# Two max tiles of a pair in one tile of two PSUM banks, reduced by one VectorE instruction, in the lead of an attention and token-mixing kernel

## The chip, the cores and the metric

The kernel runs on one core of one Trainium2 chip. The metric is device time in microseconds (us) for one execution. TensorE (PE) multiplies matrices into PSUM, which has eight banks; a bank holds 512 float32 values in each of 128 partitions, and one matmul writes within one bank. VectorE (DVE) and ScalarE (ACT) read the banks, GpSimd (POOL) works on on-chip memory, and SyncE (SP) issues the DMAs. Each engine runs its own queue in order; semaphores make one wait for another.

## The reference

A gate mixes two branches over the same input `x` (2048 tokens, 640 channels). Branch A is attention with 32 heads of 20 channels that share one key and one value head. Branch B is an MLP over the token axis with a hidden width of 1728.

```python
g = sigmoid((x * gate_w).sum(-1, keepdims=True))

# A: q has 32 heads, k and v have one
q = (x @ wq).reshape(B, S, H, Dh).transpose(0, 2, 1, 3)
k, v = x @ wk, x @ wv
p = softmax(einsum("bhqd,bkd->bhqk", q, k) * Dh ** -0.5)
a = einsum("bhqk,bkd->bhqd", p, v).transpose(0, 2, 1, 3).reshape(B, S, H * Dh) @ wo

# B: MLP over tokens
h = layernorm(x)
u = gelu(einsum("bsd,sf->bdf", h, w1) + b1)
b = (einsum("bdf,fs->bds", u, w2) + b2).transpose(0, 2, 1)

out = g * a + (1 - g) * b
```

## The kernel before

[...]

The softmax needs each row's maximum before its exponentials. So the scores are computed twice. A **max tile** (made by `ms_next`) is a 128x512 block of scores with the queries on the partitions; VectorE reduces it to one maximum per query (L500). A **score tile** (made by `qk`, called by `s_next`) is the transposed block, with the keys on the partitions; its query operand carries the row maxima as extra rows, and ScalarE takes the exponential (L652). Attention output is then collected by `pv_group` (L754). The work comes in 32 groups `n` of four heads and 512 queries. A group has 64 max tiles, 32 for each half `b` of the rows of TensorE's array. The two halves can work at the same time, on different banks.

After a first stage (projections, layer norm) comes the **lead**, the stretch that the change edits: `for fc in range(PRO)` with seven chunks of the MLP's first product. A chunk has 16 steps, and a step has six matmuls, three for each half (L686), into the two accumulators `pu`. `lead()` puts a pair of max tiles, one for each half, behind 45 of the first 106 steps. After 32 pairs, half of the 64 needed, `ms_done` takes the maxima of the group (L515), POOL negates and splits them (L517 to L519), and `store_max` and `fetch_max` turn them and send them through DRAM to the query operand. In the last chunk the numbers in `FIRST_S` name four steps behind which a first pair stands: one max tile (half 0) and one of the first four score tiles (half 1). At the end of each chunk `gelu` reads one accumulator with ScalarE (L548) and, some steps later, adds the other with VectorE (L555).

The order of instructions is written out by hand, engine by engine (`manual_schedule`), so a Python call stands where its instruction stands in its engine's queue. In the lead, banks are used in turn: `lead_bank` rotates the four banks `ms` x3 and `g`. The accumulators use `s` x2 for even chunks, and the third `s` and `o` for odd ones.

The **main stage** follows (`main`). There a small planner picks the order of tiles: each bank in `pool` has a time at which it is taken to be free, `FREE_AT` for the first ones, and `bank_take` picks the earliest. The remaining chunks of the MLP (L1035 and others) run beside max and score tiles and go to the bank `g`.

Of the kernel before, what the change touches and what calls it, by code (L numbers as in the profile page):

```python
# [17 lines left out]
P = 128  # L18
# [15 lines left out]
SIXES = range(3)  # L34
LAST_M = 2
M_FIRST = 1
FIRST_S = (4, 7, 10, 13)
NP = 12
EPS = 1e-5
GC = math.sqrt(2.0 / math.pi)  # L40
# [4 lines left out]
def mix_kernel(ctx: ExitStack, tc: tile.TileContext, A_x, A_wq, A_wk, A_wv, A_wo,  # L45
# [436 lines left out]
    def ms_next(b):  # L482
        k = given[b]
        if k >= 32 * NU:
            return None
        given[b] += 1
        n, r = divmod(k, 32)
        (kq, pr), qt = divmod(r // 4, 2), r % 4

        def step():  # L490
            if n not in mtiles:
                mtiles[n] = mpool.tile([P, 16, 4], F32, name="mp")
            ms = lead_bank() if lead_banks else bank_take()
            nc.tensor.matmul(ms, qmax[n][64 * b:64 * b + 60, pr, qt * P:(qt + 1) * P],  # L494
                             kst[64 * b:64 * b + 60, kq * NB:(kq + 1) * NB], start=True, stop=True)
            if not lead_banks:
# [3 lines left out]
            r = nc.vector.tensor_reduce(mtiles[n][:, c, kq:kq + 1], ms, axis=AX.X, op=ALU.max)  # L500
            if behind is not None:
                tc.add_manual_dep(r.ins, behind.ins.name, SYNC, reason="row tiles that share a bank")
                last["sig"] = r
            issued[b] += 1
            if min(issued) == 32 * n + 1:
                new_qmax(n + 1)

        return step

    def ms_done():  # L510
        n = len(row_max)
# [21 lines left out]
            nc.sync.dma_start(out=rows.rearrange("j p q -> j (p q)"), in_=src[b])  # L533

    chain, ahead = [], []
    lead_banks = []

    def lead_bank():
        lead_banks.append(lead_banks.pop(0))
        return lead_banks[-1]  # L540


    def gelu(d, fc, accs):
# [92 lines left out]
    def qk(u, pr, b):  # L636
        n, kb = units[u]
        assert n in back_in
        if kb == 4 and pr == 0 and b == 0:
            new_q(n + 1)  # L640
        q = qtiles[n]
        s = lead_bank() if lead_banks else bank_take()
        nc.tensor.matmul(s, kst[64 * b:64 * b + 62, kb * P:(kb + 1) * P], q[64 * b:64 * b + 62, pr, :],  # L643
                         start=True, stop=True)
        ready[u] = 0.0 if lead_banks else max(ready.get(u, 0.0), bank_give(s, "exp"))
        p = next_p()
        ptiles[u, 2 * pr + b] = p

        behind, last["ins"] = last["ins"], None

        def exp():
            e = nc.scalar.activation(p, s, AF.Exp, scale=SCALE)  # L652
# [12 lines left out]
    lead_banks.extend((*tiles[:3], ps_g.tile([P, NB], F32, name="g")))  # L665
    at, skip, final = 0, 3, NS * PRO - 6
    one_by_one[0] = True

    def lead():
        for b in range(2):  # L670
            ms_next(b)()
        ms_done()

    for fc in range(PRO):
        pu = tiles[3 + 2 * (fc % 2):5 + 2 * (fc % 2)]
        for hf in range(4):
            w1_upto(4 * fc + hf + 4)
            for f in [q_parts_due.pop(0) for _ in range(min(len(q_parts_due), 1 + fc // 5))] if fc else []:
# [142 lines left out]
    def b2_jobs(st):  # L821
        hold = {}

        def mm(fc, k, d, half):
            if not hold.get("n"):
                hold["p"], hold["n"] = ps_g.tile([P, NB], F32, name="g"), 0
# [126 lines left out]
    def a_jobs(st):  # L953
# [9 lines left out]

        def mm(c, k, d, half):
            if not hold.get("n"):
                hold["p"], hold["n"] = ps_g.tile([P, NB], F32, name="g"), 0
# [54 lines left out]
    def b1_jobs(d, fc):  # L1021
# [5 lines left out]

        def mm(st, k, half):
            if not hold.get("n"):
                hold["p"], hold["n"] = ps_g.tile([P, NB], F32, name="g"), 0  # L1030
            wh, wl = w1t[base + st // HS]
            w, h = ((wh, h_hi), (wh, h_lo), (wl, h_hi))[k]
            hold["n"] += 1
# [181 lines left out]
    spare[0] = True  # L1215
    ring[:0] = extra_p

    pool.append((lanes[0], ps_g.tile([P, NB], F32, name="g")))
    begin = lanes[0]
    while later:  # L1220
        f = later.pop(0)[1]
# [149 lines left out]
```

## Time and profile before

| what | value |
|---|---|
| median of 3 runs | 1612.38 us (1612.14 to 1612.48) |
| the profiled execution | 1611.67 us |
| span of its core | 1609.9 us |
| granted TensorE clock | 1.0 |
| TensorE busy | 1603.3 us |
| VectorE busy | 1356.4 us |
| ScalarE busy | 1309.3 us |
| POOL busy | 869.6 us |
| the lead, first to last L686 matmul | 96.4 to 159.7 us |

A row of the timeline gives the start in us from the span's start, the time taken, the engine, the line, the operation, the tile written and the tiles read, the shapes, and how many instructions were merged into the row. Matmuls are pipelined, so that TensorE looks busy while it goes slowly; the count of matmuls in a window tells more than the busy time. PE and PEld are TensorE's multiplications and its weight loads.

### The profile page before, as it was taken

How to read it: one execution, taken by the hardware profiler on the slowest of the kernel's cores; microseconds unless marked ns; L12 is line 12 of the kernel's file. 1: busy time of each engine (PE TensorE's matmuls, PEld its weight loads, DVE VectorE, ACT ScalarE, POOL GpSimd, SP SyncE). 2: the span in 40 equal slices, each digit the busy share in tenths (PEclk: the TensorE clock that was granted, in tenths of full speed). 3: DMA queues.
4: the chain of work that ended last, by engine and by line, in shares of the span. 5: the costliest groups of instructions: out<-in, count | busy, mean ns of one | idle time of the engine just before them, and what ended most of it. 6: DMA issues, size and time to landing. Idle time of an engine off the chain costs nothing.

```text
span 1609.9 us, 39500 instructions
## 1 busy us (share of the span) xinstructions
PE 1603.3 (100%) x14865; PEld 1121.9 (70%) x14865; DVE 1356.4 (84%) x2344; ACT 1309.3 (81%) x2565; POOL 869.6 (54%) x977
## 2 busy tenths in 40 slices
PE   9999999999999999999999999999999999999998
PEld 7889776677767776666666666666666666666676
DVE  6689999999999999888888888888888888766643
ACT  4545888888888888888888888888888888999974
POOL 6568766778867777644544434454544333344420
PEclk9999999999999999999999999999999999999999
DMA  7755223223233323222222122222222112245531
GB/s 215 213 164 143 78 72 81 75 76 88 75 88 84 76 64 89 64 73 81 73 69 66 54 64 70 69 73 81 73 73 69 54 51 68 87 122 180 157 95 55
DMA packets 183750, 145.07 MB, mean 90 GB/s; under 512 B 38291, under 2 KB 145424, under 8 KB 183560
## 3 DMA queue, kind: packets, MB, share of 16 engines
q1 hardware_dynamic: 183272, 142.23, 31.3%
q8 instruction: 117, 1.92, 0.5%
q14 instruction: 73, 0.60, 0.1%
q10 hardware_dynamic: 288, 0.33, 0.1%
HBM read 108.75 MB, written 32.15 MB: 88 GB/s over the span
## 4 chain that ended last, share of the span: by engine, by line
PE 98%; DVE 1%; POOL 0%; issue 0%; ACT 0%; DVEq 0%; POOLq 0%
PE s L754 16%; PE g L832 12%; PE s L643 10%; PE ms L754 10%; PE g L1035 9%; PE ms L643 8%; PE ms L494 7%; PE s L494 5%; PE pp L303 4%; PE o L754 4%; PE o L643 3%; PE o L494 2%; PE s L686 2%; PE g L971 2%; DVE mp L500 1%; PE s L926 1%
## 5 line engine op out<-in xcount | busy, mean ns | idle before, releaser
L500 DVE TENSOR_REDUCE mp<-ms 128x1 f32<-128x512 f32 x965 | 631.7, 680 | 57.6 <-PE ms L494 43.2
L652 ACT ACTIVATE p<-s 128x512 f32<-128x512 f32 x938 | 542.4, 615 | 45.4 <-PE ms L754 12.8
L500 DVE TENSOR_REDUCE mp<-s 128x1 f32<-128x512 f32 x755 | 499.4, 681 | 74.5 <-PE s L494 52.7
L652 ACT ACTIVATE p<-ms 128x512 f32<-128x512 f32 x820 | 482.2, 612 | 31.3 <-PE s L754 13.5
L767 POOL TENSOR_TENSOR acc<-acc,part 128x512 f32<-128x512 f32 x213 | 275.4, 1293 | 309.9 <-ACT part L766 297.8
L494 PE MATMUL ms<-kst,qmx 60*128 60x512 f32 x965 | 378.2, 412 | 0.1
L643 PE MATMUL s<-qst,kst 62*128 62x512 f32 x944 | 362.7, 408 | 0.2 <-DVE mp L500 0.2
L643 PE MATMUL ms<-qst,kst 62*128 62x512 f32 x826 | 323.9, 406 | 0.1
L1035 PE MATMUL g<-slot,wh 64*128 64x320 f32 x1344 | 306.0, 312 | 0.0
L494 PE MATMUL s<-kst,qmx 60*128 60x512 f32 x755 | 301.5, 413 | 0.0
L754 PE MATMUL s<-p,v_sb 128*32 128x512 f32 x2240 | 269.3, 598 | 0.0
L1035 PEld LDWEIGHTS g<-slot,wh 64*128 64x128 f32 x1344 | 216.4, 184 | 69.6 <-issue 49.5
L500 DVE TENSOR_REDUCE mp<-o 128x1 f32<-128x512 f32 x303 | 206.3, 681 | 42.8 <-PE o L494 36.9
L134 POOL TENSOR_TENSOR wl<-wr,wh 128x512 fp32r<-128x512 f32 (+1 forms) x176 | 218.3, 1240 | 30.5 <-ACT wh L131 15.4
L643 PEld LDWEIGHTS s<-qst,kst 62*128 62x128 f32 x944 | 173.3, 185 | 60.7 <-ACT p L652 27.1
L1035 PE MATMUL g<-slot,wl 64*128 64x320 f32 x672 | 205.2, 305 | 0.0
L832 PE MATMUL g<-u,wh 64*128 64x320 f32 x864 | 196.4, 309 | 0.0
L832 PE MATMUL g<-slot,wh 64*128 64x320 f32 x864 | 196.3, 309 | 0.0
L643 PEld LDWEIGHTS ms<-qst,kst 62*128 62x128 f32 x826 | 152.6, 185 | 43.8 <-ACT p L652 29.4
L494 PEld LDWEIGHTS ms<-kst,qmx 60*128 60x128 f32 x965 | 175.1, 185 | 4.2 <-DVE mp L500 0.4
L652 ACT ACTIVATE p<-o 128x512 f32<-128x512 f32 x264 | 162.3, 615 | 11.3 <-PE ms L754 7.1
L754 PE MATMUL ms<-p,v_sb 128*32 128x512 f32 x1344 | 161.6, 598 | 0.0
(251 smaller groups left out, 3081.3 us busy)
## 6 DMA issues: line engine op xcount, KB each, us to landing
wr<-in_B_w_dram SPq DMA_DIRECT2D x136, 256.0 KB
qmx<-q_scr SPq DMA_DIRECT2D x192, 80.0 KB
qst<-q_scr SPq DMA_DIRECT2D x192, 80.0 KB
ot<-l_scr SPq DMA_DIRECT2D x120, 64.0 KB
y_scr<-yo SPq DMA_DIRECT2D x16, 320.0 KB
slot<-o_scr SPq DMA_DIRECT2D x16, 320.0 KB
o_scr<-ot SPq DMA_DIRECT2D x124, 40.0 KB
o_scr<-acc SPq DMA_DIRECT2D x124, 40.0 KB
```

The costliest lines, as they stand in the source:

```text
L134: nc.gpsimd.tensor_sub(wl[:, :nv], wr[:, :nv], f32(wh[:, :nv]))
L303: nc.tensor.matmul(pp, w, t, start=first and n == 0, stop=not more and n == len(steps) - 1)
L494: nc.tensor.matmul(ms, qmax[n][64 * b:64 * b + 60, pr, qt * P:(qt + 1) * P], kst[64 * b:64 * b + 60, kq * NB:(kq + 1) * NB], start=True, s ...
L500: r = nc.vector.tensor_reduce(mtiles[n][:, c, kq:kq + 1], ms, axis=AX.X, op=ALU.max)
L643: nc.tensor.matmul(s, kst[64 * b:64 * b + 62, kb * P:(kb + 1) * P], q[64 * b:64 * b + 62, pr, :], start=True, stop=True)
L652: e = nc.scalar.activation(p, s, AF.Exp, scale=SCALE)
L686: nc.tensor.matmul(pu[r][:, :HD2], w[rows, c, :], h[rows, st, :], start=(st == 0 and k == 0), stop=(st == NS - 1 and k == 2))
L754: nc.tensor.matmul(o[32 * hh:32 * hh + 32, :], v_sb[:, kb + i, :], ptiles.pop((u, hh)), start=opened and i == 0, stop=(i == len(us) - 1) a ...
L767: nc.gpsimd.tensor_add(sums[0], sums[0], part)
L832: other_tile(half, nc.tensor.matmul(hold["p"][:, :HD2], w[r, i, :], u[d][r, fc, :], start=(hold["n"] == 1), stop=(hold["n"] == 6 * FC - 3)))
L971: other_tile(half, nc.tensor.matmul(hold["p"][:, :HD2], o[r, c, :], w[r, c, d * HD2:(d + 1) * HD2], start=(hold["n"] == 1), stop=(hold["n" ...
L1035: other_tile(half, nc.tensor.matmul(hold["p"][:, :HD2], w[r, st % HS, :], h[d][r, st, :], start=(hold["n"] == 1), stop=(hold["n"] == 6 * NS)))
```

## The change

In the lead, the four rotating banks become two tiles of two banks each, taken in turn from a pool `ps_l`. `ms_pair` replaces the two calls of `ms_next`: it issues both matmuls of a pair into the two halves of such a tile, and one VectorE instruction reduces 128x2x512 values to two maxima per partition, which it writes 32 columns apart. The pool is closed at the end of the lead, and the banks `ms` x3 and `o` are made from its four banks for the main stage.

The four first pairs no longer share the rotation. Their max tiles all use the third `s` bank, their score tiles the bank `g`, and they stand behind steps 6, 9, 12 and 15 of the last chunk instead of 4, 7, 10 and 13. The accumulators of odd chunks are the third `s` and `g` instead of the third `s` and `o`. `FREE_AT` has new numbers for the new banks.

```diff
-FIRST_S = (4, 7, 10, 13)
+FIRST_S = (6, 9, 12, 15)
...
-            ms = lead_bank() if lead_banks else bank_take()
+            ms = lead_bank() if ps_l else bank_take()
...
+    def ms_pair():
+        n = given[0] // 32
+        assert n == given[1] // 32
+        if n not in mtiles:
+            mtiles[n] = mpool.tile([P, 16, 4], F32, name="mp")
+        ms = ps_l[0].tile([P, 2, NB], F32, name="ms")
+        at = []
+        for b in range(2):
+            (kq, pr), qt = divmod(given[b] % 32 // 4, 2), given[b] % 4
+            nc.tensor.matmul(ms[:, b, :], qmax[n][64 * b:64 * b + 60, pr, qt * P:(qt + 1) * P],
+                             kst[64 * b:64 * b + 60, kq * NB:(kq + 1) * NB], start=True, stop=True)
+            at.append(((2 * b + pr) * 4 + qt) * 4 + kq)
+            given[b] += 1
+        out = mtiles[n].rearrange("p c k -> p (c k)")[:, at[0]:at[1] + 1:at[1] - at[0]]
+        nc.vector.tensor_reduce(out, ms, axis=AX.X, op=ALU.max)
+        for b in range(2):
+            issued[b] += 1
+        if min(issued) == 32 * n + 1:
+            new_qmax(n + 1)
...
-    ps_m = ctx.enter_context(tc.tile_pool(name="ps_m", bufs=3, space=PSUM))
-    ps_g = ctx.enter_context(tc.tile_pool(name="ps_g", bufs=1, space=PSUM))
-    ps_s = ctx.enter_context(tc.tile_pool(name="ps_s", bufs=3, space=PSUM))
-    ps_o = ctx.enter_context(tc.tile_pool(name="ps_o", bufs=1, space=PSUM))
-    tiles = [ps_m.tile([P, NB], F32, name="ms") for _ in range(3)]
-    tiles += [ps_s.tile([P, NB], F32, name="s") for _ in range(3)] + [ps_o.tile([P, NB], F32, name="o")]
-    lead_banks.extend((*tiles[:3], ps_g.tile([P, NB], F32, name="g")))
+    ps_g = ctx.enter_context(tc.tile_pool(name="ps_g", bufs=1, space=PSUM, side="right"))
+    ps_s = ctx.enter_context(tc.tile_pool(name="ps_s", bufs=3, space=PSUM, side="right"))
+    in_lead = ExitStack()
+    ctx.callback(in_lead.close)
+    ps_l.append(in_lead.enter_context(tc.tile_pool(name="ps_l", bufs=2, space=PSUM)))
+    g_bank = ps_g.tile([P, NB], F32, name="g")
+    s_banks = [ps_s.tile([P, NB], F32, name="s") for _ in range(3)]
+    rest_l.extend((s_banks[2], g_bank))
...
     def lead():
-        for b in range(2):
-            ms_next(b)()
+        ms_pair()
         ms_done()
...
-        pu = tiles[3 + 2 * (fc % 2):5 + 2 * (fc % 2)]
+        pu = (s_banks[2], g_bank) if fc % 2 else s_banks[:2]
...
-    FREE_AT, ACT_AT = (0.1, 0.3, 0.3, 0.6, 1.3, 0.0, 0.0), 0.5
+    FREE_AT, ACT_AT = (0.3, 0.3, 0.3, 0.6, 1.3, 0.0, 0.3), 0.5
...
-    lead_banks.clear()
+    ps_l.clear()
+    in_lead.close()
+    ps_m = ctx.enter_context(tc.tile_pool(name="ps_m", bufs=3, space=PSUM))
+    ps_o = ctx.enter_context(tc.tile_pool(name="ps_o", bufs=1, space=PSUM))
+    tiles = [ps_m.tile([P, NB], F32, name="ms") for _ in range(3)] + s_banks
+    tiles.append(ps_o.tile([P, NB], F32, name="o"))
     pool.extend(zip(FREE_AT, tiles))
```

Line numbers move: L494 (max matmul), L643 (score matmul), L652 (exp), L686 (lead matmul), L754 and L1035 become L494, L663, L672, L706, L774 and L1055; the adds of `gelu` go from L555 to L575. The pair's matmuls are L519 and its reduce is L524.

On VectorE, in the lead, behind the add of the first chunk. The numbers tell the buffers of one name apart; `mp` holds the maxima. Before:

```order
L555 TENSOR_TENSOR yo_1332<-yo_1332,s_1192 128x320
L500 TENSOR_REDUCE mp_1238<-ms_1188 128x1
L500 TENSOR_REDUCE mp_1238<-ms_1189 128x1
L500 TENSOR_REDUCE mp_1238<-ms_1190 128x1
L500 TENSOR_REDUCE mp_1238<-g_1195 128x1
```

And with the change:

```order
L575 TENSOR_TENSOR yo_1325<-yo_1325,s_1187 128x320
L524 TENSOR_REDUCE mp_1231<-ms_1365 128x2
L524 TENSOR_REDUCE mp_1231<-ms_1389 128x2
L524 TENSOR_REDUCE mp_1231<-ms_1406 128x2
L524 TENSOR_REDUCE mp_1231<-ms_1429 128x2
```

Four rows of before were two pairs in four banks; four rows now are four pairs, in two tiles in turn, each row with two results.

On VectorE, at the end of the lead, where the first pairs are mixed with the last lead pairs; the add (L555, then L575) is that of the lead's last chunk, and what follows it belongs to the main stage. Before:

```order
L500 TENSOR_REDUCE mp_1975<-ms_1188 128x1
L500 TENSOR_REDUCE mp_1975<-ms_1189 128x1
L500 TENSOR_REDUCE mp_1975<-ms_1190 128x1
L500 TENSOR_REDUCE mp_1975<-ms_1188 128x1
L555 TENSOR_TENSOR yo_2328<-yo_2328,s_1192 128x320
L500 TENSOR_REDUCE mp_1975<-s_1193 128x1
```

And with the change:

```order
L524 TENSOR_REDUCE mp_1968<-ms_2213 128x2
L500 TENSOR_REDUCE mp_1968<-s_1188 128x1
L524 TENSOR_REDUCE mp_1968<-ms_2235 128x2
L500 TENSOR_REDUCE mp_1968<-s_1188 128x1
L524 TENSOR_REDUCE mp_1968<-ms_2262 128x2
L500 TENSOR_REDUCE mp_1968<-s_1188 128x1 x2
L575 TENSOR_TENSOR yo_2321<-yo_2321,s_1187 128x320
L500 TENSOR_REDUCE mp_1968<-s_1188 128x1
```

All four first max tiles and the first max tile of the main stage now use one bank (`s_1188`), and two of their reduces stand directly ahead of the add.

On TensorE, where the lead ends and the main stage begins. Before:

```order
L686 MATMUL s_1191<-slot0_83,wl_2160 128x320
L686 MATMUL s_1192<-slot0_83,wl_2160 128x320
L1035 MATMUL g_2331<-slot0_83,wh_2207 128x320
L494 MATMUL s_1193<-kst_71,qmx_1243 128x512
L1035 MATMUL g_2331<-slot0_83,wh_2207 128x320
L643 MATMUL o_1194<-qst_1376,kst_71 128x512
```

And with the change, from the last first pair on:

```order
L706 MATMUL s_1186<-slot0_83,wl_2153 128x320
L706 MATMUL s_1187<-slot0_83,wl_2153 128x320
L494 MATMUL s_1188<-kst_71,qmx_1236 128x512
L663 MATMUL g_1185<-qst_1369,kst_71 128x512
L706 MATMUL s_1186<-slot0_83,wh_2152 128x320
L706 MATMUL s_1187<-slot0_83,wh_2152 128x320
L706 MATMUL s_1186<-slot0_83,wh_2152 128x320
L706 MATMUL s_1187<-slot0_83,wh_2152 128x320
L706 MATMUL s_1186<-slot0_83,wl_2153 128x320
L706 MATMUL s_1187<-slot0_83,wl_2153 128x320
L1055 MATMUL g_1185<-slot0_83,wh_2195 128x320
L494 MATMUL s_1188<-kst_71,qmx_1236 128x512
```

Between the last first pair (the first two rows) and the main stage's first two matmuls, which write the same two banks, `g` and the third `s`, lies one step of six matmuls. From here on both kernels have the same instructions in the same order on every engine, with other bank names: the third `s`, `ms` x3 and `o` are taken first, in this order, where it was the third `s`, `o` and `ms` x3.

More of the change, by code (lines that the diff above doesn't have):

```diff
@@ L492, in step @@
                 mtiles[n] = mpool.tile([P, 16, 4], F32, name="mp")
-            ms = lead_bank() if lead_banks else bank_take()
+            ms = lead_bank() if ps_l else bank_take()
             nc.tensor.matmul(ms, qmax[n][64 * b:64 * b + 60, pr, qt * P:(qt + 1) * P],
                              kst[64 * b:64 * b + 60, kq * NB:(kq + 1) * NB], start=True, stop=True)
-            if not lead_banks:
+            if not ps_l:
                 bank_give(ms, "max")
@@ L535, in mix_kernel @@
     chain, ahead = [], []
-    lead_banks = []
+    ps_l, rest_l = [], []
     def lead_bank():
-        lead_banks.append(lead_banks.pop(0))
-        return lead_banks[-1]
+        rest_l.append(rest_l.pop(0))
+        return rest_l[-1]
     def gelu(d, fc, accs):
@@ L641, in qk @@
         q = qtiles[n]
-        s = lead_bank() if lead_banks else bank_take()
+        s = lead_bank() if ps_l else bank_take()
         nc.tensor.matmul(s, kst[64 * b:64 * b + 62, kb * P:(kb + 1) * P], q[64 * b:64 * b + 62, pr, :],
                          start=True, stop=True)
-        ready[u] = 0.0 if lead_banks else max(ready.get(u, 0.0), bank_give(s, "exp"))
+        ready[u] = 0.0 if ps_l else max(ready.get(u, 0.0), bank_give(s, "exp"))
         p = next_p()
@@ L825, in mm @@
             if not hold.get("n"):
-                hold["p"], hold["n"] = ps_g.tile([P, NB], F32, name="g"), 0
+                hold["p"], hold["n"] = g_bank, 0
             j, i = place[fc]
@@ L965, in mm @@
             if not hold.get("n"):
-                hold["p"], hold["n"] = ps_g.tile([P, NB], F32, name="g"), 0
+                hold["p"], hold["n"] = g_bank, 0
             oT = hold["o"]
@@ L1029, in mm @@
             if not hold.get("n"):
-                hold["p"], hold["n"] = ps_g.tile([P, NB], F32, name="g"), 0
+                hold["p"], hold["n"] = g_bank, 0
             wh, wl = w1t[base + st // HS]
@@ L1216, in mix_kernel @@
     ring[:0] = extra_p
-    pool.append((lanes[0], ps_g.tile([P, NB], F32, name="g")))
+    pool.append((lanes[0], g_bank))
     begin = lanes[0]
```

## The prediction

> **What bounds the kernel now.** I read the page's totals and its chain first, then the lead (the stretch that the change edits) in windows of about one chunk, then the chain of that stretch alone, then single rows.
>
> ```profile
> span 1609.9 us, 39500 instructions
> ...
> PE 1603.3 (100%) x14865; PEld 1121.9 (70%) x14865; DVE 1356.4 (84%) x2344; ACT 1309.3 (81%) x2565; POOL 869.6 (54%) x977
> ...
> PE 98%; DVE 1%; POOL 0%; issue 0%; ACT 0%; DVEq 0%; POOLq 0%
> ```
>
> TensorE is the chain: 98% of it. Work on another engine matters only where TensorE stands still for it. The page gives VectorE 1% of the chain, some 16 us, so the question is how much of that lies in the lead. The windows show time, then busy us and count of each engine.
>
> ```profile
> 105.00:114.00 9.00, 9.00 (x118) 8.72 (x116) 9.00 (x17) 4.98 (x10) 5.80 (x5) 1.00 0.49 137
> ...
> 132.00:141.00 9.00, 9.00 (x118) 8.94 (x116) 8.97 (x17) 5.00 (x11) 7.69 (x10) 1.00 0.49 135
> 141.00:150.00 9.00, 8.89 (x111) 8.50 (x109) 8.97 (x17) 4.95 (x10) 8.17 (x9) 1.00 0.59 156
> 150.00:159.80 9.80, 9.45 (x103) 8.17 (x101) 9.05 (x16) 6.00 (x13) 6.50 (x7) 1.00 0.49 129
> ```
>
> VectorE (third pair) is busy without a gap from 105 us on. TensorE's busy time hides what happens, its count does not: 118 matmuls in 9 us until 141, then 111, then 103 in 9.8 us. The chain of that stretch says who held it (start, us, what):
>
> ```profile
> 141.45 1.17 DVE mp L500 x2
> ...
> 143.02 6.80 DVE mp L500 x12
> ...
> 151.78 4.80 DVE mp L500 x8
> ```
>
> From 141 to 156.6 us the chain runs through the max reduces (L500), not through TensorE. How much is lost there follows from TensorE's pace while it was free:
>
> ```profile
> 99.42 0.46 PE L686 MATMUL s<-slot,wh 64*128 64x320 f32 x4
> ...
> 99.86 0.45 PE L686 MATMUL s<-slot,wh 64*128 64x320 f32 x4
> ...
> 100.31 0.39 PE L494 MATMUL ms<-kst,qmx 60*128 60x512 f32 x1
> ...
> 100.54 0.46 PE L686 MATMUL s<-slot,wh 64*128 64x320 f32 x4
> ...
> 101.65 0.46 PE L686 MATMUL s<-slot,wh 64*128 64x320 f32 x4
> ...
> 103.20 0.46 PE L686 MATMUL s<-slot,wh 64*128 64x320 f32 x4
> ```
>
> A step of six matmuls takes 99.86 - 99.42 = 0.44 us. A pair of max tiles adds 0.23: from 101.65 to 103.20 lie three steps and a pair, 1.55 - 1.32 = 0.23. The lead has 7 x 16 = 112 steps, 45 lead pairs and four first pairs (a max tile and a score tile): 112 x 0.44 + 49 x 0.23 = 60.6 us. It took from 96.4 us to the first matmul of the main stage:
>
> ```profile
> L686 PEld LDWEIGHTS s<-slot,wh x352: 183/184/188, 96.4 to 159.4; 64*128 64x128 f32 x176
> ...
> 159.84 0.45 PE L1035 MATMUL g<-slot,wh 64*128 64x320 f32 x2
> ```
>
> That is 63.4 us, so 2.9 us are lost to VectorE. This is all that a faster VectorE can give in the lead: 0.18% of the time.
>
> **The change, part by part.**
>
> *One reduce for two banks.* 45 instructions of 128x1024 replace 90 of 128x512. The trace has none of the new shape.
>
> ```profile
> 107.00 0.47 DVE L555 TENSOR_TENSOR yo<-yo,s 128x320 f32<-128x320 f32 x1
> 107.39 1.88 DVE L500 TENSOR_REDUCE mp<-ms 128x1 f32<-128x512 f32 x3
> 109.19 0.68 DVE L500 TENSOR_REDUCE mp<-g 128x1 f32<-128x512 f32 x1
> 109.79 1.87 DVE L500 TENSOR_REDUCE mp<-ms 128x1 f32<-128x512 f32 x3
> ...
> 139.79 0.22 DVE L515 TENSOR_REDUCE mm<-mp 128x16 f32<-128x64 f32 x1
> ```
>
> A single reduce lasts 0.68 us, but the next starts 0.60 after it (107.39 to 109.79 are four). Against the 64-element reduce of sixteen groups (0.22) the slope is 0.46 / 448 = 1.03 ns per element, and sixteen groups cost nothing that shows. So 512 more elements add 0.53: a pair lasts 1.21 and occupies 1.13. Two singles occupy 1.20. The bounds are 1.07 (twice the slope, no fixed part) and 1.36 (two times 0.68, nothing overlapped). I take 1.13, since both rows that fix it are reduces with the same output. Per chunk of 16 steps with 7 pairs, VectorE needs 14 x 0.60 + 0.39 (L555, 107.00 to 107.39) = 8.8 us now, TensorE 16 x 0.44 + 7 x 0.23 = 8.65: VectorE falls behind by some 0.1 per chunk, and the last chunk adds four more reduces. With the change it needs 7 x 1.13 + 0.39 = 8.3 and waits for TensorE. The backlog is gone and with it the 2.9 us, except where one of the following takes some back.
>
> [...]
>
> *Two tiles of two banks instead of four of one.* A pair is freed only when its whole reduce is done. The hand-over is seen here:
>
> ```profile
> 99.19 0.39 PE L494 MATMUL ms<-kst,qmx 60*128 60x512 f32 x2
> ...
> 99.62 1.89 DVE L500 TENSOR_REDUCE mp<-ms 128x1 f32<-128x512 f32 x3 [1.21 <-PE ms L494]
> ...
> 150.11 1.27 DVE L500 TENSOR_REDUCE mp<-ms 128x1 f32<-128x512 f32 x2
> ...
> 151.48 0.47 PE L643 MATMUL ms<-qst,kst 62*128 62x512 f32 x1
> ```
>
> 0.43 from a matmul's start to its reduce, 0.1 from the reduce's end to the next writer (151.38 to 151.48). A pair's tile is therefore busy 0.43 + 1.21 + 0.1 = 1.74 us. TensorE returns to it two pairs later, after at least four steps and two pairs, 2.2 us. So 0.4 us of lateness is free, and a lone L555 (0.39) fits in. One place doesn't: behind the row max of the first group VectorE's queue holds the transpose of L526, which waits for POOL.
>
> ```profile
> 140.98 0.23 POOL L519 TENSOR_TENSOR mn<-mm,mn 128x16 fp32r<-128x16 f32 x1
> ...
> 141.24 0.21 DVE L526 STREAM_TRANSPOSE mt<-mn 128x32 f32<-128x32 f32 x1
> ```
>
> It starts 0.03 after POOL. Today VectorE arrives at about the same moment, being behind; with the change it arrives some 0.5 us earlier and stands, and the pair reduces queue behind it. After the free 0.4 I charge 0.15 us to TensorE.
>
> *Own banks for the first four pairs.* Their max tile always uses the third score bank, the score tile the `g` bank, three steps apart. On TensorE that is three steps, a first pair and mostly a lead pair: 1.32 + 0.46 = 1.78 us. The max tile needs 0.43 + 0.68 + 0.1 = 1.2, plus up to 1.13 when a pair's reduce stands ahead of it, 2.3 in all: up to 0.55 lost, three times at most. Walking both queues forward from the durations above gives about 0.45 once and 0.1 once; I charge 0.6.
>
> *Set later (6, 9, 12, 15).* The last score tile is issued one step before the lead's end, and the main stage's first matmul writes the same `g` bank.
>
> ```profile
> 156.62 0.49 PE L643 MATMUL g<-qst,kst 62*128 62x512 f32 x1
> ...
> 157.16 0.60 ACT L652 ACTIVATE p<-g 128x512 f32<-128x512 f32 x1 [1.78 <-PE g L643]
> ...
> 159.92 0.53 ACT L548 ACTIVATE yo<-s,bias 128x320 f32<-128x320 f32 x1 [0.30 <-PE s L686]
> ...
> 160.54 0.49 DVE L555 TENSOR_TENSOR yo<-yo,s 128x320 f32<-128x320 f32 x1 [1.33 <-POOL wl L134]
> 160.94 0.68 DVE L500 TENSOR_REDUCE mp<-s 128x1 f32<-128x512 f32 x1
> ...
> 161.68 0.49 PE L643 MATMUL s<-qst,kst 62*128 62x512 f32 x1 [0.22 <-DVE mp L500]
> ...
> 164.50 1.92 PE L754 MATMUL s<-p,v_sb 128*32 128x512 f32 x16
> ```
>
> A score tile's exp ends 0.54 + 0.60 = 1.14 us after its matmul starts, and that start is 0.44 + 0.23 = 0.67 before the lead's end. So the first matmul of the main stage waits some 0.45 us, which it doesn't today. But today TensorE stops 1.84 us into the main stage anyway (161.68), for L548, then L555, then a reduce. That run of three starts later by a few tenths, since L548 now stands behind the last exp; TensorE's late start fills the gap that was there. I charge 0.05, with 0.8 as the far end (both in full).
>
> The queues of SP and POOL keep their order. On ScalarE the first of the four exps moves from ahead of a weight copy (L131) to behind it, and that copy is for a chunk that TensorE reaches some 5 us later: nothing. The first score tile needs a DMA (L533), which TensorE will ask for at step 6 without stalls, 151.3 us by the paces above, about where it asks today (151.48): nothing.
>
> *The main stage* keeps its order, instruction for instruction, with other bank names, so it keeps its pace. Behind the attention matmuls it is TensorE's alone:
>
> ```profile
> 170.45 1.92 PE L754 MATMUL s<-p,v_sb 128*32 128x512 f32 x16
> 176.41 1.92 PE L754 MATMUL s<-p,v_sb 128*32 128x512 f32 x16
> ```
>
> A round takes 5.96 us whatever came before: what the lead gains reaches the end in full.
>
> **Sum:** 2.9 - 0.15 - 0.6 - 0.05 = 2.1, less 0.1 for VectorE's small gaps around L515: 2.0 us. The profiled execution (1611.67, its span 1609.9) would become 1609.7; it lies 0.7 under the median shown, 1612.38, which becomes 1610.4. This is 0.12%, less than the 0.2% that a measurement of this kernel can tell from no change.
>
> **Rivals.**
>
> *Nothing saved by the wide reduce.* Pairs start 1.20 apart, like two singles. VectorE keeps its 8.8 us per chunk; only the first four pairs' own banks help, which part of the stalls of 151.48 pays for, some 0.8: 1611.6. For it: no row has a reduce over two banks. Against: the small cost of L515. [...]
>
> *The wide reduce is dearer than two* (slower). At the far bound, 1.36, VectorE needs 7 x 1.36 + 0.39 = 9.9 per chunk against 8.65, 1.26 lost in each of six chunks and 0.5 in the last: 8.1 against 2.9 now, 1617.6. It decides from about 1.22 on, and passes 0.2% at about 1.29. For it: crossing a bank and the coarser hand-over are in no row. Against: the slope.
>
> *Handed back at the entry.* Both waits there count in full, 0.8: 1611.2.
>
> *Everything comes free* (faster). Nothing of the 2.9 is taken back, and the main stage's first round, 4.66 us (159.84 to 164.50) for 17 tiles of 0.23 = 3.9, loses its 0.75 too: 3.65, 1608.7. Against: its run of L548, L555 and reduces stays.
>
> **Chances.** Forecast 0.49 (own range 1609.6 to 1611.0), entry 0.13, nothing saved 0.13, dearer 0.11 (0.10 of it beyond 0.2%), all free 0.14. So faster 0.14, same 0.76, slower 0.10. The range runs from 1608.8 to 1613.0: it leaves out half of the free case and the dearer one, 0.18.
>
> **What would show it.** Right: rows of L524 with 1.2 us each, starting at least 1.13 apart; idle time on VectorE between 105 and 141 us; the first L1055 near 158.0, the first L774 near 162.6; rounds of 5.96. Wrong: L524 over 1.25 us apart; matmul counts under 118 per 9 us before 141; a first round over 5 us; a main stage with another pace, which nothing here foresees.

## The result

The changed kernel takes 1609.88 us (median of 22 runs, 1609.6 to 1610.45), the kernel before 1612.18 (22 runs, 1611.52 to 1612.94). The ratio is 0.9987, its 95% interval 0.9981 to 0.9992: 2.3 us less, somewhere from 1.3 to 3.1. The profiled executions are 1.47 us apart, 1610.20 against 1611.67.

In the last piece of order shown with the change, the last first pair is the third and fourth row, L494 and L663, not the first two.

The page of the changed kernel, its totals and the engines' shares of the chain:

```profile
span 1608.4 us, 39456 instructions
...
PE 1602.2 (100%) x14865; PEld 1121.2 (70%) x14865; DVE 1354.3 (84%) x2299; ACT 1309.1 (81%) x2565; POOL 868.5 (54%) x977
...
PE 97%; DVE 1%; SPq 1%; DMA 0%; POOL 0%; issue 0%; ACT 0%; DVEq 0%; POOLq 0%
```

The 1% of SPq is SyncE's queue issuing DMAs in the first 12 us, before the lead. There are 45 VectorE instructions fewer (2344 to 2299), and only 2.1 us of VectorE's 1356 us of busy time are gone: a pair's reduce is one instruction, but nearly as long as two overlapped ones (1.22 us, where two singles in a row took 1.27). The lead in the same windows as before (time, then busy us and count of PE, PEld, DVE, ACT, POOL, the granted clock, DMA):

```profile
105.00:114.00 9.00, 9.00 (x118) 8.72 (x116) 8.73 (x9) 4.83 (x10) 5.83 (x5) 1.00 0.47 130
...
132.00:141.00 9.00, 9.00 (x118) 8.72 (x116) 8.65 (x10) 5.26 (x11) 7.81 (x11) 1.00 0.49 128
141.00:150.00 9.00, 9.00 (x118) 8.60 (x116) 9.00 (x10) 4.97 (x10) 8.21 (x8) 1.00 0.64 161
150.00:158.00 8.00, 7.84 (x96) 7.15 (x92) 7.41 (x10) 5.65 (x12) 6.14 (x7) 1.00 0.55 141
```

VectorE now has 0.3 us of idle time in 9 until 141, where it had none, and TensorE issues 118 matmuls from 141 to 150 as everywhere else, where it had 111. The new reduces as a group (ns, minimum, median, maximum), and VectorE's rows around the first row max (start, us; a row with x4 or x7 holds so many):

```profile
L524 DVE TENSOR_REDUCE mp<-ms x45: 1183/1217/1228, 99.8 to 155.5; 128x2 f32<-128x1024 f32 x45
```

```profile
133.38 4.61 DVE L524 TENSOR_REDUCE mp<-ms 128x2 f32<-128x1024 f32 x4
...
138.25 1.23 DVE L524 TENSOR_REDUCE mp<-ms 128x2 f32<-128x1024 f32 x1 [0.26 <-PE ms L519]
139.52 0.22 DVE L535 TENSOR_REDUCE mm<-mp 128x16 f32<-128x64 f32 x1
139.65 1.22 DVE L524 TENSOR_REDUCE mp<-ms 128x2 f32<-128x1024 f32 x1
140.92 0.21 DVE L546 STREAM_TRANSPOSE mt<-mn 128x32 f32<-128x32 f32 x1
141.06 1.18 DVE L524 TENSOR_REDUCE mp<-ms 128x2 f32<-128x1024 f32 x1
142.16 0.48 DVE L575 TENSOR_TENSOR yo<-yo,s 128x320 f32<-128x320 f32 x1
142.55 8.01 DVE L524 TENSOR_REDUCE mp<-ms 128x2 f32<-128x1024 f32 x7
...
157.86 0.69 DVE L500 TENSOR_REDUCE mp<-s 128x1 f32<-128x512 f32 x1 [0.59 <-PE g L663]
159.00 0.49 DVE L575 TENSOR_TENSOR yo<-yo,s 128x320 f32<-128x320 f32 x1 [0.45 <-PE g L1055]
```

One wide reduce lasts 1.22 us, and the next starts 1.13 after it: seven in a row take 8.01, so (8.01 - 1.22) / 6 = 1.13. At 138.25 VectorE waits 0.26 us for TensorE, which it did nowhere between 105 and 141 us before. TensorE's rows where the lead ends and where the first attention matmuls start (`wh` and `wl` are the high and the low part of the MLP's weights):

```profile
153.39 0.32 PE L706 MATMUL s<-slot,wl 64*128 64x320 f32 x2
153.87 0.49 PE L494 MATMUL s<-kst,qmx 60*128 60x512 f32 x1 [0.16 <-DVE mp L500]
...
157.97 0.31 PE L706 MATMUL s<-slot,wl 64*128 64x320 f32 x2
158.55 0.41 PE L1055 MATMUL g<-slot,wh 64*128 64x320 f32 x1 [0.28 <-ACT p L672]
...
162.96 1.92 PE L774 MATMUL s<-p,v_sb 128*32 128x512 f32 x16
...
168.90 1.92 PE L774 MATMUL s<-p,v_sb 128*32 128x512 f32 x16
```

The last two matmuls of the lead start at 157.97 and would be followed 0.15 later, at 158.12; the main stage's first one comes at 158.55, 0.43 late, for the last exp. A round behind it takes 5.94 us (5.96 before).

From these rows, and their like in every kernel below, four stretches (us): the lead, up to where the main stage's first matmul could start; its wait; from it to the first L774 (L754 before); from there to the end.

| kernel | lead | wait | first round | sum of the three | rest |
|---|---|---|---|---|---|
| before | 63.40 | 0 | 4.66 | 68.05 | 1445.40 |
| changed | 61.52 | 0.43 | 4.41 | 66.36 | 1445.47 |
| changed, again | 61.51 | 0.43 | 4.41 | 66.36 | 1445.74 |

The gain is 1.69 us, all of it ahead of the first attention matmul. The rest moves by hundredths or tenths, and not with the change: it lies between 1445.3 and 1445.7 in all twelve profiles of this study. So the traces say 1.7, the medians 2.3 with an interval that holds 1.7.

### The profile page after: what moved, and what is told of

It reads as the page before. It is cut to its first block, busy times and chain, and to the rows that moved or that the text cites. A ratio compares the mean times of both kernels' runs of the same rounds, so it can differ in the third digit from the quotient of the medians.

```text
span 1608.4 us, 39456 instructions
## 1 busy us (share of the span) xinstructions
PE 1602.2 (100%) x14865; PEld 1121.2 (70%) x14865; DVE 1354.3 (84%) x2299; ACT 1309.1 (81%) x2565; POOL 868.5 (54%) x977
## 4 chain that ended last, share of the span: by engine, by line
PE 97%; DVE 1%; SPq 1%; DMA 0%; POOL 0%; issue 0%; ACT 0%; DVEq 0%; POOLq 0%
PE s L774 16%; PE g L852 11%; PE ms L774 11%; PE s L663 10%; PE g L1055 9%; PE ms L663 8%; PE ms L494 6%; PE s L494 6%; PE pp L303 4%; PE o L663 3%; PE o L494 2%; PE s L706 2%; PE o L774 2%; PE g L991 2%; PE s L946 1%; DVE mp L524 1%
## 5 line engine op out<-in xcount | busy, mean ns | idle before, releaser
L500 DVE TENSOR_REDUCE mp<-ms 128x1 f32<-128x512 f32 x889 | 582.3, 681 | 80.0 <-PE ms L494 71.0
L672 ACT ACTIVATE p<-s 128x512 f32<-128x512 f32 x938 | 543.2, 617 | 45.4 <-PE ms L774 13.0
L672 ACT ACTIVATE p<-ms 128x512 f32<-128x512 f32 x807 | 471.7, 614 | 30.6 <-PE s L774 11.7
L663 PE MATMUL s<-qst,kst 62*128 62x512 f32 x944 | 362.9, 407 | 0.0
L494 PE MATMUL ms<-kst,qmx 60*128 60x512 f32 x889 | 357.4, 416 | 0.0
L663 PE MATMUL ms<-qst,kst 62*128 62x512 f32 x811 | 319.6, 407 | 0.0
L1055 PE MATMUL g<-slot,wh 64*128 64x320 f32 x1344 | 306.1, 312 | 0.3 <-ACT p L672 0.3
L494 PE MATMUL s<-kst,qmx 60*128 60x512 f32 x759 | 303.6, 413 | 0.2 <-DVE mp L500 0.2
L774 PE MATMUL s<-p,v_sb 128*32 128x512 f32 x2240 | 269.3, 598 | 0.0
L1055 PEld LDWEIGHTS g<-slot,wh 64*128 64x128 f32 x1344 | 216.4, 184 | 70.1 <-issue 50.3
L500 DVE TENSOR_REDUCE mp<-o 128x1 f32<-128x512 f32 x308 | 209.8, 681 | 18.5 <-PE o L494 14.4
L663 PEld LDWEIGHTS s<-qst,kst 62*128 62x128 f32 x944 | 173.4, 185 | 60.6 <-ACT p L672 27.8
L1055 PE MATMUL g<-slot,wl 64*128 64x320 f32 x672 | 205.3, 305 | 0.0
L774 PE MATMUL ms<-p,v_sb 128*32 128x512 f32 x1560 | 189.6, 598 | 0.0
L663 PEld LDWEIGHTS ms<-qst,kst 62*128 62x128 f32 x811 | 150.2, 185 | 55.4 <-ACT p L672 28.5
L672 ACT ACTIVATE p<-o 128x512 f32<-128x512 f32 x274 | 169.1, 617 | 11.6 <-PE ms L774 5.6
L494 PEld LDWEIGHTS ms<-kst,qmx 60*128 60x128 f32 x889 | 164.0, 185 | 3.6
```

The costliest lines, as they stand in the source:

```text
L774: nc.tensor.matmul(o[32 * hh:32 * hh + 32, :], v_sb[:, kb + i, :], ptiles.pop((u, hh)), start=opened and i == 0, stop=(i == len(us) - 1) a ...
L1055: other_tile(half, nc.tensor.matmul(hold["p"][:, :HD2], w[r, st % HS, :], h[d][r, st, :], start=(hold["n"] == 1), stop=(hold["n"] == 6 * NS)))
```

## The experiments

Each differs from the changed kernel by the lines shown; e7 is the changed kernel itself, and e8 differs from the kernel before. The medians beside a kernel are of runs on the same chip. The table gives them together; "sum" is the sum of the three stretches above, and the ratio's interval is at 95%.

| kernel | lead | wait | sum | against before's 68.05 | median, before's median | ratio |
|---|---|---|---|---|---|---|
| e1_four_banks | 62.77 | 0.44 | 67.61 | -0.44 | 1611.46, 1612.08 | 0.9996 (0.9987 to 1.0006) |
| e2_split | 62.78 | 0.43 | 67.63 | -0.42 | 1611.31, 1612.08 | 0.9995 (0.9985 to 1.0004) |
| e4_half | 60.85 | 0.41 | 65.67 | -2.38 | 1609.67, 1612.08 | 0.9984 (0.9974 to 0.9993) |
| e5_dear | 67.64 | 0.44 | 72.50 | +4.45 | 1615.57, 1612.08 | 1.0022 (1.0012 to 1.0031) |
| e5b_dear | 65.13 | 0.43 | 69.98 | +1.93 | 1613.61, 1612.04 | 1.0009 (0.9999 to 1.0018) |
| e3_early | 62.78 | 0 | 67.55 | -0.50 | 1610.95, 1612.04 | 0.9992 (0.9982 to 1.0001) |
| e6_mid | 61.96 | 0 | 66.74 | -1.31 | 1610.45, 1612.04 | 0.9990 (0.9981 to 1.0000) |
| e7_again | 61.51 | 0.43 | 66.36 | -1.69 | 1610.09, 1612.04 | 0.9987 (0.9978 to 0.9997) |
| e8_late_alone | 63.02 | 0 | 67.85 | -0.20 | 1611.74, 1611.82 | 0.9999 (0.9989 to 1.0008) |
| e9_sooner | 61.69 | 0.41 | 66.50 | -1.55 | 1609.98, 1611.82 | 0.9989 (0.9980 to 0.9999) |

The timed ratios alone don't separate most of these from each other; the stretches of the traces do, since the changed kernel, profiled twice, gave the same sum to 0.01 us. Of the others there is one profile each.

### The two parts taken apart: e1_four_banks, e2_split

e1 has the own banks and the later places, but four banks of one and two single reduces for a pair:

```diff
-        ms = ps_l[0].tile([P, 2, NB], F32, name="ms")
+        ms = [ps_l[0].tile([P, NB], F32, name="ms") for _ in range(2)]
...
-            nc.tensor.matmul(ms[:, b, :], qmax[n][64 * b:64 * b + 60, pr, qt * P:(qt + 1) * P],
+            nc.tensor.matmul(ms[b], qmax[n][64 * b:64 * b + 60, pr, qt * P:(qt + 1) * P],
...
-        out = mtiles[n].rearrange("p c k -> p (c k)")[:, at[0]:at[1] + 1:at[1] - at[0]]
-        nc.vector.tensor_reduce(out, ms, axis=AX.X, op=ALU.max)
+        flat = mtiles[n].rearrange("p c k -> p (c k)")
+        for b in range(2):
+            nc.vector.tensor_reduce(flat[:, at[b]:at[b] + 1], ms[b], axis=AX.X, op=ALU.max)
...
-    ps_l.append(in_lead.enter_context(tc.tile_pool(name="ps_l", bufs=2, space=PSUM)))
+    ps_l.append(in_lead.enter_context(tc.tile_pool(name="ps_l", bufs=4, space=PSUM)))
```

> The changed kernel with its banks and places for the first four pairs, but each pair of max tiles goes to two one-bank tiles (four in turn) and is reduced by two instructions, as before the change. Theory (the gain is the 0.06 us that each pair saves on VectorE): VectorE is behind again, matmul counts under 118 per 9 us between 123 and 150 us, the lead takes 62.4 us (61.5 with the change, 63.4 before it), the time is 0.8 to 1.0 us under the kernel before. Rival (the gain comes from the own banks and later places of the first four pairs): the lead stays at 61.5 us and the time 2 us under the kernel before.

e2 keeps the tiles of two banks and has two single reduces in each:

```diff
-        out = mtiles[n].rearrange("p c k -> p (c k)")[:, at[0]:at[1] + 1:at[1] - at[0]]
-        nc.vector.tensor_reduce(out, ms, axis=AX.X, op=ALU.max)
+        flat = mtiles[n].rearrange("p c k -> p (c k)")
+        for b in range(2):
+            nc.vector.tensor_reduce(flat[:, at[b]:at[b] + 1], ms[:, b, :], axis=AX.X, op=ALU.max)
```

> As the run with four one-bank tiles, but the pair keeps its tile of two banks, and the two reduces read one half each; the tile is free when both are done. What differs from that run is the coarser hand-over alone. Theory: 0 to 0.3 us longer than with four one-bank tiles (62.4 to 62.7 us in the lead), since TensorE comes back to a tile 2.2 us later and the tile is busy for 1.8. Rival (the coarser hand-over is dear and the wide reduce pays for it): 1 us or more longer in the lead.

Both lose 1.25 us of the 1.69 again. With the own banks and the later places in place, the wide instruction is therefore worth 1.25. The tile of two banks costs no more than 0.02 by itself (67.63 against 67.61), so the coarser hand-over that the prediction put at nothing shows as nothing here. The leads of 62.77 and 62.78 are 0.3 to 0.4 longer than the theory of e1 had, and far from its rival's 61.5. e1's window of the stretch in which before lost matmuls:

```profile
141.00:150.00 9.00, 8.90 (x111) 8.50 (x110) 8.97 (x18) 4.97 (x10) 8.15 (x9) 1.00 0.60 161
```

111 matmuls, as in the kernel before. A pair is 0.07 dearer on VectorE (1.20 against 1.13), VectorE has no idle time to speak of (busy for 8.97 of these 9 us), and TensorE waits for it.

### How much there was to gain: e4_half

```diff
-        nc.vector.tensor_reduce(out, ms, axis=AX.X, op=ALU.max)
+        nc.vector.tensor_reduce(out, ms[:, :, :NB // 2], axis=AX.X, op=ALU.max)
```

> The changed kernel, whose lead reduces read only the first 256 columns of each bank (half of the keys of the row maxima is left out), so that a pair costs VectorE about 0.6 us less. It shows what the lead takes when VectorE never holds TensorE. Theory: 60.6 us for the lead (112 steps of 0.44 and 49 pairs of 0.23), 0.9 us less than with the change; the wait of 0.43 us at the main stage's first matmul stays; the time is 2.5 to 3.0 us under the kernel before. Rival (TensorE's pace in the lead has another bound, such as weights or DMA): the lead stays at 61.5 us.

Its reduces as a group, and VectorE's share (third pair) of the windows:

```profile
L524 DVE TENSOR_REDUCE mp<-ms x45: 692/694/696, 99.4 to 154.2; 128x2 f32<-128x512 f32 x45
```

```profile
105.00:141.00 36.00, 36.00 (x460) 34.85 (x460) 22.24 (x36) 20.55 (x42) 30.56 (x31) 1.00 0.54 149
141.00:150.00 9.00, 9.00 (x118) 8.72 (x116) 5.44 (x9) 5.30 (x12) 8.04 (x8) 1.00 0.79 180
```

VectorE is busy for 60%, and the lead still takes 60.85 us. That is TensorE's own time for it: no step is longer than 0.45 us without a pair and 0.68 with one, apart from the very first (0.55) and the one with two pairs (0.91). It is 0.25 more than the 60.6 worked out from the steps, and the time is 2.4 us under the kernel before, a little less than expected. A faster pair could give another 61.52 - 60.85 = 0.67 in the lead and no more.

The same comparison, chunk by chunk, shows where VectorE holds TensorE. A chunk's time runs from its first matmul to that of the next, the last one's to where the main stage's first matmul could start. The kernels e3 and e8 are described further below. The sixth chunk of the changed kernel and of e4, for example, lies between these rows:

```profile
139.61 0.30 PE L706 MATMUL s<-slot,wh 64*128 64x320 f32 x1
...
148.41 0.45 PE L706 MATMUL s<-slot,wh 64*128 64x320 f32 x4
```

```profile
139.23 0.30 PE L706 MATMUL s<-slot,wh 64*128 64x320 f32 x1
...
147.90 0.45 PE L706 MATMUL s<-slot,wh 64*128 64x320 f32 x4
```

| kernel | chunk 1 | 2 to 4 | 5 | 6 | 7 |
|---|---|---|---|---|---|
| before | 8.32 | 8.67, 8.67, 8.68 | 8.74 | 9.24 | 11.07 |
| e8_late_alone | 8.32 | 8.67, 8.67, 8.68 | 8.74 | 9.23 | 10.70 |
| e1_four_banks | 8.32 | 8.67, 8.67, 8.69 | 8.73 | 9.24 | 10.44 |
| e3_early | 8.32 | 8.67 each | 8.67 | 8.80 | 10.96 |
| changed | 8.32 | 8.67 each | 8.67 | 8.80 | 9.70 |
| e4_half | 8.32 | 8.67 each | 8.67 | 8.67 | 9.16 |

Three quarters of what the kernel before loses lies in the last chunk (11.07 - 9.16 = 1.91 of 2.55), and 0.57 more in the sixth.

The row of L524 shows a second thing: two results of 256 elements each last 0.694 us, one of 512 lasts 0.682 (e1's 90 reduces). The second result and the second bank together cost 0.012.

### What a dearer pair costs: e5_dear, e5b_dear

A small reduce of constants behind each wide one makes a pair dearer:

```diff
         nc.vector.tensor_reduce(out, ms, axis=AX.X, op=ALU.max)
+        nc.vector.tensor_reduce(idle, ident[:, :64].rearrange("p (c k) -> p c k", k=4), axis=AX.X, op=ALU.max)
...
+    idle = ev.tile([P, 16], F32, name="idle")
```

> The changed kernel with one more small VectorE instruction behind each pair's reduce (128x16 from 128x64 of a constant, 0.14 us from start to start), so that a pair occupies VectorE for 1.27 us in place of 1.13. Theory (the lead is bound by VectorE once a pair passes about 1.2): 7 x 1.27 + 0.39 = 9.3 us per chunk against TensorE's 8.65, so the lead takes 65.5 us, 4 us more than with the change, and the time is 1.5 to 2.5 us over the kernel before. Rival (VectorE has more slack than reckoned): under 1 us more than with the change.

The first try measured something else beside it. What the added line waited for, from the answer on that line, and VectorE's rows:

```profile
  DMA q_scr<-xa: 2.4, 1
```

```profile
104.68 1.22 DVE L524 TENSOR_REDUCE mp<-ms 128x2 f32<-128x1024 f32 x1
105.81 0.21 DVE L525 TENSOR_REDUCE idle<-ident 128x16 f32<-128x64 f32 x1
105.94 1.22 DVE L524 TENSOR_REDUCE mp<-ms 128x2 f32<-128x1024 f32 x1
```

The scratch tile had got memory that a DMA still read from, and its first user stood 2.4 us for that, with all pairs behind it. The lead took 67.64 us instead of the 65.5 expected, and the time was 3.5 us over the kernel before. In the next kernel the tile has memory of its own:

```diff
+    idle = const.tile([P, 16], F32, name="idle")
...
         nc.vector.tensor_reduce(out, ms, axis=AX.X, op=ALU.max)
+        nc.vector.tensor_reduce(idle, ident[:, :64].rearrange("p (c k) -> p c k", k=4), axis=AX.X, op=ALU.max)
```

> The run with the extra small VectorE instruction again, with its scratch tile in memory that no earlier DMA uses: there, the first of the small instructions stood 2.4 us behind a DMA. Theory: a pair with the small instruction occupies 1.26 us (104.68 to 105.94 in that run), so the chunk needs 9.2 us against 8.65; the lead and the wait behind it take 65.5 to 66.0 us, 2 us less than in that run, and the time is 1.5 to 2.5 us over the kernel before. Rival (the lead slows down more than VectorE's own time accounts for): 68 us again, 3.5 us over the kernel before.

```profile
103.41 1.22 DVE L525 TENSOR_REDUCE mp<-ms 128x2 f32<-128x1024 f32 x1
104.55 0.21 DVE L526 TENSOR_REDUCE idle<-ident 128x16 f32<-128x64 f32 x1
104.67 1.22 DVE L525 TENSOR_REDUCE mp<-ms 128x2 f32<-128x1024 f32 x1
```

Pairs start 1.26 apart, and the sum rises from 66.36 to 69.98, that is above before. Lead and wait take 65.56 us, as the theory has it. A chunk in which VectorE sets the pace would need 7 x 1.26 + 0.39 = 9.21 us, and the third to the fifth take 9.20. By the durations of the prediction a pair costs TensorE nothing up to (8.65 - 0.39) / 7 = 1.18. Above that lie e2 (1.20 apart, 67.63) and e5b (1.26 apart, 69.98); on the line between them before's 68.05 is reached at 1.21. That is an estimate from two points, and the prediction put the turn at about 1.22. A gain of 0.07 us on a pair was worth having only because VectorE and TensorE stood within 2% of each other (8.8 against 8.65).

### The places of the first pairs: e3_early, e6_mid, e8_late_alone

```diff
-FIRST_S = (6, 9, 12, 15)
+FIRST_S = (4, 7, 10, 13)
```

> The changed kernel with the first four pairs behind steps 4, 7, 10 and 13 again, with their own banks. It tells the later places from the rest. Theory: no wait at the main stage's first matmul (0.43 us with the change), but more waits for the shared bank in the last chunk, since the lead pairs still run there: the lead takes 62.3 to 62.6 us in place of 61.5, the first round 4.7 in place of 4.85, together 0.6 to 0.9 us more than with the change. Rival (the later places cost more at the main stage's start than they save): 0.2 to 0.4 us less than with the change.

e3 is the changed kernel with the old places. It loses 1.19 of the 1.69, more than the 0.6 to 0.9 expected. VectorE's rows and TensorE's:

```profile
154.35 2.35 DVE L524 TENSOR_REDUCE mp<-ms 128x2 f32<-128x1024 f32 x2
156.61 0.68 DVE L500 TENSOR_REDUCE mp<-s 128x1 f32<-128x512 f32 x1
```

```profile
150.98 0.47 PE L663 MATMUL g<-qst,kst 62*128 62x512 f32 x1 [0.32 <-DVE yo L575]
...
157.34 0.50 PE L494 MATMUL s<-kst,qmx 60*128 60x512 f32 x1 [0.74 <-DVE mp L500]
```

The first max tiles have one bank. Where they stand among the last lead pairs, a max tile's reduce queues behind two wide ones (154.35 to 156.61), the bank is not free, and TensorE stands 0.74 for it; 0.32 more went to the `g` bank, which the add of the chunk before still read. The last lead pair stands behind step 10 of the chunk: of the old places one comes after it, of the new ones two.

e6 takes the places between:

```diff
-FIRST_S = (6, 9, 12, 15)
+FIRST_S = (5, 8, 11, 14)
```

> The changed kernel with the first four pairs behind steps 5, 8, 11 and 14. Theory: no wait at the main stage's first matmul, the lead 61.8 to 62.0 us, the first round 4.7: together 0.2 to 0.5 us more than with the change. Rival (the wait at the main stage's start is what is left to gain): 0.2 to 0.4 us less than with the change, and the best of all.

It lies between, 0.38 above the changed kernel. Its lead is 0.45 longer, and its main stage starts without a wait; yet the first round then lasts 4.78, little less than the 0.43 + 4.41 = 4.84 of the changed kernel. The wait for the last exp is nearly free, since a gap stood behind it anyway.

e8 is the kernel before with the new places alone:

```diff
-FIRST_S = (4, 7, 10, 13)
+FIRST_S = (6, 9, 12, 15)
```

> The kernel before, with the first four pairs behind steps 6, 9, 12 and 15 and nothing else of the change: four shared banks in rotation and single reduces. With it the parts are told apart: wide reduces with early places gave 67.55 us from the lead's first matmul to the first attention matmul, single reduces with own banks and late places 67.61, all together 66.36, the kernel before 68.05. Theory (the parts pay only together, since VectorE's backlog at the lead's end is what TensorE waits for, and either part alone leaves most of it): 67.6 to 68.1 us, at most 0.5 less than before. Rival (the later places are worth over 1 us by themselves): under 67.0 us.

It gains 0.20 in its trace, and nothing that the times can tell. The windows of 150 to 157.5 of three kernels, in the order before, e8, changed, show the last chunk by its count of matmuls:

```profile
150.00:157.50 7.50, 7.15 (x74) 5.87 (x72) 7.50 (x14) 3.91 (x9) 5.92 (x6) 1.00 0.51 133
```

```profile
150.00:157.50 7.50, 7.34 (x79) 6.24 (x77) 7.50 (x14) 4.75 (x10) 6.04 (x6) 1.00 0.56 138
```

```profile
150.00:157.50 7.50, 7.34 (x90) 6.70 (x88) 7.27 (x9) 5.55 (x11) 5.64 (x7) 1.00 0.53 132
```

74, 79 and 90. Late places alone give 0.20 us of the sum; late places with own banks 0.44 (e1); wide reduces with own banks at the old places 0.50 (e3); all three 1.69. The chunks above show which part acts where: the wide reduce brings the fifth and sixth chunk near to TensorE's own time, with the old places too, and the last chunk falls to 9.70 only with all three. The parts pay in full only together. That each of the others leaves a wait at the same queue fits the rows of e3, but own banks by themselves were not run, nor the wide reduce with the first pairs still in the rotation of the lead's banks: its tiles have two banks, a first max tile needs one.

### Once more, and one step on: e7_again, e9_sooner

e7 is the changed kernel unaltered.

> The changed kernel as it is, profiled a second time, to see how far the lead and the first round repeat. Theory: from the lead's first matmul to the first attention matmul 66.4 us within 0.1 (61.5 in the lead and 4.85 behind it), 1.7 us less than before the change; what the runs show beyond that lies outside the lead, in the spread between executions. Rival (the rest of the kernel gains too): a second profile whose main stage is shorter than that of the kernel before by 0.5 us or more.

Lead, wait and first round come out the same to 0.01 us; the rest took 1445.74 instead of 1445.47, with the same instructions. The medians now differ by 1.95 us instead of 2.3. So no trace shows a gain in the main stage that would account for what the medians have beyond 1.7; it is put down to the spread between executions, and both intervals hold 1.7.

e9 ends the lead pairs three steps sooner, so that fewer of them meet the first pairs:

```diff
-    at, skip, final = 0, 3, NS * PRO - 6
+    at, skip, final = 0, 3, NS * PRO - 9
```

> The changed kernel with its 45 lead pairs ended three steps sooner (spread over 100 steps, not 103), so that fewer of them stand between the first four pairs. Theory (what the last chunk still loses, 0.7 us over the run with half reduces, is VectorE's queue there): 66.1 to 66.3 us from the lead's first matmul to the first attention matmul, against 66.36; too little to see in the time. Rival (the pairs being closer, 1.2 us apart where VectorE needs 1.13 and the adds of gelu, VectorE falls behind again): over 66.6 us.

66.50: neither the 66.1 to 66.3 hoped for nor above 66.6. VectorE has 35.53 us of work from 105 to 141 instead of 34.86, since the same 45 pairs stand closer. The last chunk has one lead pair less, and yet takes 9.71 us, where the changed kernel takes 9.70: TensorE still waits there for the one bank of the first max tiles. Rows of VectorE and of TensorE:

```profile
152.21 1.21 DVE L524 TENSOR_REDUCE mp<-ms 128x2 f32<-128x1024 f32 x1
153.34 0.67 DVE L500 TENSOR_REDUCE mp<-s 128x1 f32<-128x512 f32 x1
```

```profile
154.07 0.49 PE L494 MATMUL s<-kst,qmx 60*128 60x512 f32 x1
```

The reduce of the first max tile stands behind a wide one, ends at 154.01, and the next max tile starts at 154.07. Not better than the changed kernel.

## Why the prediction came out right

The forecast was 1610.4 us, 2.0 less than before; it is 1609.88, 2.3 less, and 1.7 in the traces. Of its rivals, "nothing saved" (1611.6) and "dearer" (1617.6) fall by the rows of L524, "handed back at the entry" by the first round, and "everything comes free" by the last chunk (9.70 against 9.16) and the entry. The signs that it named for being right came: reduces of 1.22 us that start 1.13 apart, idle time on VectorE before 141 us, rounds of 5.94. The first L1055 and the first L774 came later than named, at 158.55 and 162.96 instead of 158.0 and 162.6. Term by term (us, + is gained):

| step | predicted | measured | from |
|---|---|---|---|
| what VectorE cost the lead | +2.9 | +2.55 | 63.40 - 60.85 (e4_half) |
| the transposes that wait for POOL | -0.15 | -0.13 | sixth chunk, 8.80 against 8.67 (e4_half) |
| own banks for the first pairs | -0.6 | -0.54 | last chunk, 9.70 against 9.16 (e4_half) |
| entry of the main stage | -0.05 | -0.18 | 0.43 + 4.41 against 4.66 |
| small gaps of VectorE around the row max | -0.1 | in the -0.13 | the first five chunks are as in e4_half |
| sum | +2.0 | +1.70 | 68.05 - 66.36 = 1.69 |

So the mechanism was right, apart from the worth of the places (below), and the losses came where they were expected. Two sizes were off, the first term by 0.35 and the entry by 0.13, and smaller errors took back part of it. That the timed gain (2.3, in the second series 1.95) lies as near to 2.0 as it does is in part luck: the traces show 1.7.

**The price of the wide reduce** was the step on which all hung: 1.21 long and 1.13 apart were worked out from the 512-element and the 64-element reduce, 1.217 and 1.13 are measured. That sixteen groups cost nothing that shows held for two as well (0.012). The next reduce starts 0.09 before the end of a wide one, as it started 0.08 before the end of a single one.

**The lead's loss** was 0.35 too large. TensorE's own time for the lead came out of six rows around 100 us, as 0.44 per step and 0.23 per pair; over the whole lead it is 60.85 instead of 60.6. In e4_half a step without a pair takes 0.442 on the mean, which makes some 0.2 over 112 steps, and the first step takes 0.1 more than the others.

**The transposes** cost TensorE 0.13, together with the small gaps around the row max, where 0.15 and 0.1 had been charged, and VectorE's stand was shorter than thought. Counted from the lead's first matmul, VectorE came to the row max 0.4 us sooner than before (139.52 - 96.59 against 139.79 - 96.44), but POOL's split came sooner with it: VectorE was free at 139.65 + 1.13 = 140.78 and L546 starts at 140.92, 0.14 later. The row max, this stand, the transpose and the add (L575) together made the reduces late. TensorE's pairs behind them:

```profile
141.60 0.39 PE L519 MATMUL ms<-kst,qmx 60*128 60x512 f32 x2
142.71 0.39 PE L519 MATMUL ms<-kst,qmx 60*128 60x512 f32 x2
143.82 0.50 PE L519 MATMUL ms<-kst,qmx 60*128 60x512 f32 x2
```

The reduce of the pair of 141.60 starts at 142.55, 0.95 after it instead of 0.43, so it is 0.52 late; with the 0.4 that the prediction reckoned as free, 0.12 is left. The reduce ends at 143.77. The third pair, which takes the same tile, starts at 143.82 and lasts 0.11 longer than the others. The count of 118 matmuls from 141 to 150 is too coarse to show that. The chunks ahead of it have the same add and pairs, but neither row max nor transpose, and lose nothing (8.67 us for each of the second to the fifth, as in e4_half).

**Own banks** cost 0.54, all of it in the last chunk. The step with the first pair at 153.87 takes 1.12 us, in e4_half 0.68; 0.33 of it is seen ahead of the pair (0.48 after the matmuls of 153.39, instead of 0.15). The step with the last first pair takes 0.79, in e4_half 0.67. That is 0.44 once and 0.12 once, where the prediction had 0.45 once and 0.1 once.

**The entry** was the term that was sized worst beside its own size: the wait is 0.43 as worked out (0.45), but the run of L568, L575 and the reduce took back less of it than thought. L575 starts 0.89 us after the lead's end (159.00), in the kernel before 0.70 (160.54). So 0.18 arrives at the first attention matmul and not 0.05; it is far from the 0.8 of the rival.

**What the prediction had no price for** is the places by themselves. It counted them as a small loss at the entry (0.05), and worked out the own banks' loss of 0.6 with the places as given. e3 shows what stands behind this: at the old places the own banks would have cost 1.3 more in the lead (62.78 - 61.52), so the later places are worth 1.19 of the sum, and the wide reduce 1.25. The sum came out because the prediction walked both queues forward with all three edits in place. What one edit is worth depends on the others: the places bring 0.20 alone and 1.19 on top of the other two.

**The main stage** kept its pace (5.94 us a round, 5.96 before), so what the lead gained reached the end, as forecast.

## What to carry to other kernels

- Where one engine stands a few per cent above the engine that it feeds, a gain of 6% on its commonest instruction (1.20 to 1.13) is worth most of what is to be gained, here 1.25 of 1.69 us, and 5% the other way (1.26) costs 1.9: work out the need of both per chunk, 8.8 against 8.65 here, before counting instructions.
- Where the instruction sits in its engine's queue is worth as much as its price (1.19 us here, against 1.25): with one bank per role, place an instruction that needs it where no long one stands ahead of it. Price edits on one queue together, by walking it, not one by one.
- For an experiment that adds work, give its scratch data memory that nothing used before; in e5_dear its first user stood 2.4 us behind a DMA.

## What the hardware showed that was not expected

- One VectorE reduce reads two banks in one instruction, 2 x 512 values, and pays nothing that shows for crossing: 1.217 us, 0.535 more than for 512 (0.682), or 1.04 ns per element, where the prediction's slope within a bank is 1.03. Two results from two banks instead of one from one cost 0.012.
- Giving a tile back in pieces or as a whole made no difference of more than 0.02 us (e1 against e2), with the next writer two pairs away.
- A scratch tile from a shared pool held up its first user for 2.4 us, because a DMA still read what had been in that memory (e5_dear): a wait that no line of the added code shows.
